# Attention and MLP in one kernel: in the first unit ACT's casts of x and of the heads are placed behind exponentials

## The chip, the cores and the metric

The kernel runs on one core of a Trainium2 chip. The metric is the device time of one execution in microseconds, the median of the runs shown. A profiled execution gives the rows below; its times are in microseconds from the start of its span.

Engine names: PE is TensorE (PEld its weight loads), ACT is ScalarE, DVE is VectorE, POOL is GpSimd, SP is SyncE, which issues the transfers (SPq is its queue).

## The reference

```python
scores = scale * np.matmul(q, k.transpose(0, 1, 3, 2))      # B=4, H=8, S=768, D=64
keep = is_sink | in_window                                  # first 4 keys, and the last 128
scores = np.where(keep, scores, -1000000000.0)
a = np.exp(scores - np.max(scores, axis=-1, keepdims=True))
a = a / (np.sum(a, axis=-1, keepdims=True) + 1e-09)
x = np.matmul(a, v)                                         # -> (3072 tokens, 512)
h = x @ w_in                                                # 512 -> 2048
g = np.maximum(0.01 * h, h)
out = (g @ w_out).astype(np.float32)                        # 2048 -> 512
```

## The kernel before, in words

The work is cut into eight units, one for each batch and half of its sequence, of 384 queries each. A unit has eight heads, taken in four pairs, and each head has three query blocks j = 0, 1, 2 of 128 rows. Only the keys of a block's window and the four sinks are multiplied.

One block goes through these steps. PE multiplies the scores into PSUM (L321, tile s). DVE adds the mask and takes the row's minimum of the negated scores (L341). ACT takes the exponential with its row sum (L345). DVE adds the small constant and takes the reciprocal of the sum (L346, L347) and scales the row into pk (L351). PE transposes pk (L376, tile t), and ACT copies the result to pt (L379). For unit 0 the transposes share a single PSUM tile, so a transpose waits for the copy of the one before it. When a pair is through, its sink columns are transposed too (L419), and PE multiplies pt by the values (L457, tile v). ACT rounds the result, x, to the matmul type as xh (L519, in emit_x), and DVE forms the rest xl (L520).

A head's queries and keys reach SBUF as qkraw. They are used in two parts, a rounded one and a rest: split_head has ACT cast qkraw into qksp (L278), and POOL then subtracts for the rest, in two instructions (L279, L281). Heads 0 and 1 of unit 0 are used unsplit. qksp has two buffers, so the cast for head h+2 waits until the scores of head h are done. The tag qkraw has one buffer, and in unit 0 the odd heads have one of their own, qkraw2. From unit 1 on every head uses qkraw, so there the transfer of a head can be issued only when POOL has finished the split of the head before. The calls are these:

```python
nxt = following(u, h)
if u < WIDE and j == min(nxt[0], 1):
    split_next(u, h)      # cast of the following head
```

So a head of unit 0 has its successor split right after its block 0, and head 7 of unit 0 has the first head of unit 1 split after its block 1.

The MLP of a unit runs one unit behind the attention. Its weights come as 64-bit words, which DVE packs to floats (L175, L177, L179), ACT rounds (L183: wih, woh) and POOL subtracts (L184: wil, wol). A step has twelve matmuls of h (L573), ACT's scaling (L580), DVE's maximum (L581), ACT's cast gh (L582), DVE's rest gl (L583), and nine matmuls of o (L594). There is one PSUM tile for h, so the next step's matmuls wait for the maximum.

PE's order is written out by the two streams of the program and stays as written, with short dummy matmuls in unit 0 (L311). The order on ACT, DVE, POOL and SP is chosen by a scheduler, which places each instruction where its own timeline finds it ready. Every engine takes its instructions in the order that results, and so does SP with its transfers.

## Time and profile before

| | us |
|---|---|
| median of 3 runs | 744.82 (744.72 to 745.72) |
| the profiled execution's own time | 745.67 |
| its span | 743.7 |
| PE busy | 718.4 |
| DVE busy | 562.2 |
| ACT busy | 433.3 |
| POOL busy | 381.3 |

The span is what the rows cover; the execution's own time has about 2 us around it. A busy time is the sum over an engine's instructions. The page's granted clock of PE is a share of full speed, 2.4 GHz; a half is the other level, 1.2 GHz.

### The profile page before, as it was taken

To read this page: it belongs to the slowest core of one execution; us is meant where nothing else is said; L and a number is where in the kernel's file an instruction comes from. 1 tells how busy PE (TensorE), PEld (TensorE's weight loads), DVE (VectorE), ACT (ScalarE), POOL (GpSimd) and SP (SyncE) were. 2 spreads that over 40 slices of the span, in tenths; PEclk is the share of its full clock that TensorE was granted. 3 is DMA by queue.
4 is the path that set the end of the run, shared out by engine and by line. 5 is a ranking of instruction groups with operands and counts; after the bars stand their busy time and mean duration, and the time that the engine had idled before them with its cause. 6 is when DMAs were issued, how large, how long until landed. Compare 5 with 4: busy or idle time off the path is not lost.

```text
span 743.7 us, 12694 instructions
## 1 busy us (share of the span) xinstructions
PE 718.4 (97%) x3935; PEld 623.0 (84%) x3935; DVE 562.2 (76%) x1832; ACT 433.3 (58%) x1208; POOL 381.3 (51%) x490
## 2 busy tenths in 40 slices
PE   8879999989999999999999999999999999999996
PEld 4547777769999988999988988999988999988995
DVE  7776889877667888888888888888888978733222
ACT  5567667657666566666566666666666655522221
POOL 3554455555445677665666577665666555300000
PEclk9989999999999999999999999999999999999998
DMA  6443565643121343324333343324331321001001
GB/s 209 163 133 125 187 203 189 186 141 100 58 57 62 115 125 122 90 92 154 115 108 109 130 125 109 98 93 150 120 107 49 107 69 44 1 1 42 1 1 46
DMA packets 30474, 76.94 MB, mean 103 GB/s; under 512 B 3584, under 2 KB 9152, under 8 KB 30400
## 3 DMA queue, kind: packets, MB, share of 16 engines
q1 hardware_dynamic: 30256, 75.94, 32.5%
q8 instruction: 33, 0.54, 0.3%
q14 instruction: 41, 0.34, 0.1%
q10 hardware_dynamic: 144, 0.13, 0.1%
HBM read 69.76 MB, written 6.29 MB: 102 GB/s over the span
## 4 chain that ended last, share of the span: by engine, by line
PE 83%; DVE 8%; ACT 5%; issue 2%; DMA 1%; POOL 1%; SPq 0%; ACTq 0%; DVEq 0%
PE o L594 32%; PE h L573 32%; PE v L457 9%; PE s L321 5%; PE t L389 2%; DVE gl L583 2%; PE warm L311 1%; PE t L376 1%; ACT qksp L278 1%; DVE zeroi L196 1%; ACT s L345 1%; DVE pk L351 1%; DMA qkraw<-in_qk 1%; DVE g L581 1%; ACT pk L345 0%
## 5 line engine op out<-in xcount | busy, mean ns | idle before, releaser
L573 PE MATMUL h<-xh,wih 128*128 128x384 f32 x512 | 187.6, 366 | 1.5 <-DVE g L581 1.3
L573 PE MATMUL h<-xh,wil 128*128 128x384 f32 x512 | 172.8, 338 | 1.5 <-POOL wil L184 1.5
L573 PE MATMUL h<-xl,wih 128*128 128x384 f32 x512 | 172.4, 337 | 0.0
L594 PE MATMUL o<-woh,gh 128*128 128x512 f32 x384 | 154.2, 402 | 0.0
L594 PE MATMUL o<-woh,gl 128*128 128x512 f32 x384 | 151.2, 394 | 0.0
L594 PE MATMUL o<-wol,gh 128*128 128x512 f32 x384 | 151.0, 393 | 0.0
L360 POOL TENSOR_SCALAR_AFFINE_SELECT pt<-stg 128x256 fp32r<-128x256 f32 x240 | 101.4, 447 | 83.3 <-DVE stg L402 67.8
L279 POOL TENSOR_TENSOR qksp<-qkraw,qksp 64x524 fp32r<-64x524 f32 (+1 forms) x62 | 74.9, 1208 | 112.9 <-issue 65.7
L583 DVE TENSOR_TENSOR gl<-g,gh 128x384 fp32r<-128x384 f32 x128 | 105.8, 827 | 17.3 <-ACT gh L582 15.8
L581 DVE TENSOR_TENSOR g<-h,g 128x384 f32<-128x384 f32 x128 | 71.0, 555 | 60.2 <-ACT g L580 58.0
L573 PEld LDWEIGHTS h<-xh,wih 128*128 128x128 f32 x512 | 96.5, 188 | 16.0 <-issue 2.9
L580 ACT ACTIVATE g<-h 128x384 f32<-128x384 f32 x128 | 62.2, 486 | 69.6 <-PE h L573 69.0
L345 ACT ACTIVATE pk<-pk,negm 128x128 f32<-128x128 f32 (+2 forms) x168 | 70.3, 418 | 55.7 <-DVE negm L341 54.7
L573 PEld LDWEIGHTS h<-xl,wih 128*128 128x128 f32 x512 | 96.9, 189 | 3.0
L573 PEld LDWEIGHTS h<-xh,wil 128*128 128x128 f32 x512 | 96.2, 188 | 1.8 <-POOL wil L184 1.8
L594 PEld LDWEIGHTS o<-woh,gl 128*128 128x128 f32 x384 | 72.0, 188 | 16.3 <-DVE gl L583 0.2
L582 ACT CAST gh<-g 128x384 fp32r<-128x384 f32 x128 | 65.7, 513 | 32.9 <-DVE g L581 30.6
L594 PEld LDWEIGHTS o<-woh,gh 128*128 128x128 f32 x384 | 72.4, 189 | 11.2 <-issue 2.4
L321 PEld LDWEIGHTS s<-qksp 128*128 128x128 f32 x372 | 68.8, 191 | 13.7 <-issue 5.0
L321 PE MATMUL s<-qksp 128*128 128x260 f32 (+1 forms) x372 | 77.1, 289 | 2.4 <-DVE negm L341 2.4
L594 PEld LDWEIGHTS o<-wol,gh 128*128 128x128 f32 x384 | 72.3, 188 | 6.5
L281 POOL TENSOR_TENSOR qksp<-qkraw,qksp 128x384 fp32r<-128x384 f32 x62 | 67.9, 1095 | 4.7
(124 smaller groups left out, 1218.8 us busy)
## 6 DMA issues: line engine op xcount, KB each, us to landing
qkraw<-in_qk SPq DMA_DIRECT2D x32, 454.0 KB, 3.2
qkraw<-in_qk SPq DMA_DIRECT2D x30, 388.0 KB, 3.5
wiraw<-in_w_in SPq DMA_DIRECT2D x16, 512.0 KB, 3.7
woraw<-in_w_out SPq DMA_DIRECT2D x16, 512.0 KB, 3.6
ciraw<-in_w_in SPq DMA_DIRECT2D x16, 512.0 KB, 3.5
coraw<-in_w_out SPq DMA_DIRECT2D x16, 512.0 KB, 3.6
out<-ob SPq DMA_DIRECT2D x23, 256.0 KB, 2.0
vraw<-in_vu SPq DMA_DIRECT2D x12, 256.0 KB, 2.6
```

The lines of the kernel that those rows point to most:

```text
L279: nc.gpsimd.tensor_tensor(out=sp[D:P, TU:TU + n], in0=raw[D:P, TU:TU + n], in1=sp[D:P, TU:TU + n].bitcast(F32), op=ALU.subtract)
L281: nc.gpsimd.tensor_tensor(out=sp[:, TU + n:2 * TU + n], in0=raw[:, 0:TU], in1=sp[:, 0:TU].bitcast(F32), op=ALU.subtract)
L321: nc.tensor.matmul(ps[:, 0:kn], lhsT=sp[rows, off + j * P:off + (j + 1) * P], rhs=sp[rows, TU + k0:TU + k0 + kn], start=c == 0, stop=c == ...
L345: nc.scalar.activation(out=e, in_=e, func=AF.Exp, scale=-1.0, bias=neg, accum_out=sm)
L360: nc.gpsimd.affine_select(out=out, in_=src, pattern=([[0, x]] if x > 1 else []) + [[sign, P]], base=-1 if prev else 0, channel_multiplier= ...
L457: nc.tensor.matmul(out[:, o:o + m], lhsT=l, rhs=r, start=c == 0, stop=c == len(mms) - 1, skip_group_check=True)
L573: nc.tensor.matmul(ph[:, 0:TU], lhsT=w[:, cs], rhs=x, start=cc == 0 and c == 0, stop=cc == NCC - 1 and c == 2)
L580: nc.scalar.mul(g, ph[:, 0:TU], 0.01)
L581: anchor[0] = nc.vector.tensor_tensor(out=g, in0=ph[:, 0:TU], in1=g, op=ALU.max)
L582: nc.scalar.copy(out=gh, in_=g)
L583: (nc.gpsimd if u == 0 and fc % 4 < GLP else nc.vector).tensor_tensor(out=gl, in0=g, in1=gh.bitcast(F32), op=ALU.subtract)
L594: nc.tensor.matmul(po[t], lhsT=gg[:, tsl], rhs=w, start=f == 0 and c == 0, stop=f == NFC - 1 and c == 2)
```

## The change

The program keeps a list of its exponentials. A helper, behind_exp, gives an instruction the rule that it may not stand ahead of a named earlier exponential on its engine. It is used for two casts. The cast of x (emit_x), in unit 0 alone, is placed behind the latest exponential that has been written. The cast of a head (split_head) is placed behind the one before the latest, while the program is in unit 0. Nothing is added to or removed from the work, and the rule itself is an order, not a wait.

```diff
--- before.py
+++ after.py
@@ -153,6 +153,7 @@
     mlp_steps = NFC * (NCC + T)
     wts = {}
     anchor = [None]
+    exps = []
 
     def raw_words(nm, fc, name):
         raw = iopool.tile([P, 512, 2], I32, tag="wraw", name=name, bufs=2)
@@ -269,13 +270,19 @@
             sps[nxt] = split_head(*nxt)
             pump()
 
+    def behind_exp(u, back, f):
+        if u == 0 and len(exps) >= back:
+            with tc.issue_after(exps[-back].ins):
+                return f()
+        return f()
+
     def split_head(u, h):
         half = u % 2
         n = NK[half]
         raw = raws.pop((u, h))
         rawbusy.discard(raw_place(u, h)[1])
         sp = apool.tile([P, 2 * TU + NK[1]], F32R, tag="qksp", name=f"qksp{u}_{h}")
-        nc.scalar.copy(out=sp[:, 0:TU + n], in_=raw[:, 0:TU + n])
+        behind_exp(phase["unit"], 2, lambda: nc.scalar.copy(out=sp[:, 0:TU + n], in_=raw[:, 0:TU + n]))
         nc.gpsimd.tensor_tensor(out=sp[D:P, TU:TU + n], in0=raw[D:P, TU:TU + n],
                                 in1=sp[D:P, TU:TU + n].bitcast(F32), op=ALU.subtract)
         nc.gpsimd.tensor_tensor(out=sp[:, TU + n:2 * TU + n], in0=raw[:, 0:TU],
@@ -342,7 +349,7 @@
                                                    scale=-SCALE, scalar=3.0e38, op0=ALU.add, op1=ALU.min,
                                                    accum_out=neg)
         sm = apool.tile([P, 1], F32, tag="sm", name=f"sm{u}_{h}_{j}", bufs=4)
-        nc.scalar.activation(out=e, in_=e, func=AF.Exp, scale=-1.0, bias=neg, accum_out=sm)
+        exps.append(nc.scalar.activation(out=e, in_=e, func=AF.Exp, scale=-1.0, bias=neg, accum_out=sm))
         nc.vector.tensor_scalar(out=sm, in0=sm, scalar1=1e-9, scalar2=None, op0=ALU.add)
         nc.vector.reciprocal(out=sm, in_=sm)
         if NACT >> u & 1:
@@ -516,7 +523,7 @@
     def emit_x(u, pair, x):
         xh = xpool.tile([P, TU], F32R, tag=f"xh{pair}", name=f"xh{u}_{pair}")
         xl = xpool.tile([P, TU], F32R, tag=f"xl{pair}", name=f"xl{u}_{pair}")
-        nc.scalar.copy(out=xh, in_=x)
+        behind_exp(u, 1, lambda: nc.scalar.copy(out=xh, in_=x))
         (nc.gpsimd if u < XLP and not native_values(u, 2 * pair) else nc.vector).tensor_tensor(out=xl, in0=x, in1=xh.bitcast(F32), op=ALU.subtract)
         xs[u].append((xh, xl))
```

The scheduler runs with these rules and orders the four engines anew; PE's order is unchanged. In the rows below, names end in numbers: s0_3_1 is unit 0, head 3, block 1, and the last number is a buffer's.

On ACT, around the cast of x of the first pair, the order before is this (xh0_0 is the cast of x, qksp0_5 that of head 5):

```order
L519 CAST xh0_0_382<-v0_0_342 128x384
L382 COPY sk0_1_259<-pk0_2_260 128x2x4
L278 CAST qksp0_5_417<-qkraw0_5_275 128x776
L345 ACTIVATE s0_3_0_349,sm0_3_0_353<-s0_3_0_349,negm_65 128x128
L379 COPY pt0_2_261<-t9_399 128x256
L345 ACTIVATE s0_3_1_369,sm0_3_1_373<-s0_3_1_369,negm_65 128x260
L345 ACTIVATE s0_3_2_390,sm0_3_2_394<-s0_3_2_390,negm_65 128x260
L379 COPY pt0_2_261<-t10_423 128x256
```

and with the change:

```order
L389 COPY sk0_1_259<-pk0_2_260 128x2x4
L352 ACTIVATE s0_3_0_349,sm0_3_0_353<-s0_3_0_349,negm_65 128x128
L386 COPY pt0_2_261<-t9_399 128x256
L352 ACTIVATE s0_3_1_369,sm0_3_1_373<-s0_3_1_369,negm_65 128x260
L526 CAST xh0_0_382<-v0_0_342 128x384
L386 COPY pt0_2_261<-t10_423 128x256
L352 ACTIVATE s0_3_2_390,sm0_3_2_394<-s0_3_2_390,negm_65 128x260
L285 CAST qksp0_5_417<-qkraw0_5_275 128x776
```

The cast of x has moved behind two exponentials of head 3 and a copy, and head 5's cast behind all three exponentials.

On ACT, at the end of unit 0, the twelve rows from the cast of unit 1's head 0 (qksp1_0) to that of its head 1 (qksp1_1) are these before:

```order
L278 CAST qksp1_0_662<-qkraw1_0_508 128x908
L345 ACTIVATE s0_6_2_601,sm0_6_2_605<-s0_6_2_601,negm_65 128x260
L379 COPY pt0_6_553<-t22_648 128x128
L183 CAST wih2_619<-wi2_614 128x512
L519 CAST xh0_2_672<-v0_4_632 128x384
L382 COPY sk0_3_551<-pk0_6_552 128x2x4
L345 ACTIVATE s0_7_0_639,sm0_7_0_643<-s0_7_0_639,negm_65 128x128
L379 COPY pt0_6_553<-t23_689 128x256
L345 ACTIVATE s0_7_1_653,sm0_7_1_657<-s0_7_1_653,negm_65 128x260
L345 ACTIVATE s0_7_2_680,sm0_7_2_684<-s0_7_2_680,negm_65 128x260
L379 COPY pt0_6_553<-t24_707 128x256
L278 CAST qksp1_1_732<-qkraw1_1_666 128x908
```

and with the change:

```order
L285 CAST qksp1_0_662<-qkraw1_0_508 128x908
L386 COPY pt0_6_553<-t23_689 128x256
L352 ACTIVATE s0_7_1_653,sm0_7_1_657<-s0_7_1_653,negm_65 128x260
L526 CAST xh0_2_672<-v0_4_632 128x384
L352 ACTIVATE s0_7_2_680,sm0_7_2_684<-s0_7_2_680,negm_65 128x260
L184 CAST woh2_628<-wo2_623 128x512
L386 COPY pt0_6_553<-t24_707 128x256
L389 COPY sk0_3_551<-pk0_7_637 128x2x4
L352 ACTIVATE pk1_0_696,sm1_0_0_702<-pk1_0_696,negm_65 128x260
L386 COPY pt0_7_638<-t25_714 128x128
L356 ACTIVATE pk1_0_696<-pk1_0_696,sm1_0_0_702 128x260
L285 CAST qksp1_1_732<-qkraw1_1_666 128x908
```

Head 0's cast stood ahead of the exponential of head 6, block 2, and now stands behind that of head 7, block 0. Head 1's cast stood ahead of the copy to pt0_7 from t25. It now stands behind that copy, and the next row behind it is the copy to pt0_7 from t26.

On SP, the transfers around qkraw1_1, which feeds that cast, are these before:

```order
L159 DMA wiraw3_676<-in_w_in 128x1024
L222 DMA qkraw1_1_666<-in_qk1 128x908
L246 DMA vn1_2_957<-in_vu1 128x512
L247 DMA vn1_2_957<-in_vs 24x128
L159 DMA woraw3_678<-in_w_out 128x1024
```

and with the change:

```order
L160 DMA wiraw3_676<-in_w_in 128x1024
L247 DMA vn1_2_957<-in_vu1 128x512
L248 DMA vn1_2_957<-in_vs 24x128
L160 DMA woraw3_678<-in_w_out 128x1024
L223 DMA qkraw1_1_666<-in_qk1 128x908
```

The transfer of head 1 was the second of these and is now the last, behind the weights woraw3.

On POOL, in unit 1, where the MLP has begun, the order before is this (wil6 is the rest of the weights of MLP step 6):

```order
L184 TENSOR_TENSOR wol5_1012<-wo5_1006,woh5_1011 128x512
L279 TENSOR_TENSOR qksp1_5_1277<-qkraw1_5_1128,qksp1_5_1277 64x524
L281 TENSOR_TENSOR qksp1_5_1277<-qkraw1_5_1128,qksp1_5_1277 128x384
L184 TENSOR_TENSOR wil6_1084<-wi6_1078,wih6_1083 128x512
L184 TENSOR_TENSOR wol6_1093<-wo6_1087,woh6_1092 128x512
L184 TENSOR_TENSOR wil7_1177<-wi7_1171,wih7_1176 128x512
```

and with the change:

```order
L185 TENSOR_TENSOR wol5_1012<-wo5_1006,woh5_1011 128x512
L185 TENSOR_TENSOR wil6_1084<-wi6_1078,wih6_1083 128x512
L286 TENSOR_TENSOR qksp1_5_1277<-qkraw1_5_1128,qksp1_5_1277 64x524
L288 TENSOR_TENSOR qksp1_5_1277<-qkraw1_5_1128,qksp1_5_1277 128x384
L185 TENSOR_TENSOR wol6_1093<-wo6_1087,woh6_1092 128x512
L185 TENSOR_TENSOR wil7_1177<-wi7_1171,wih7_1176 128x512
```

The rest wil6 has moved ahead of both subtractions of head 5.

## Rows read from the trace of the kernel before

**Rows 1.** Part 1 of the page: engine, busy us, share, instructions.
```profile
PE 718.4 (97%) x3935; PEld 623.0 (84%) x3935; DVE 562.2 (76%) x1832; ACT 433.3 (58%) x1208; POOL 381.3 (51%) x490
```

**Rows 2.** PE's timeline, unit 0: start, us, line, instruction, count, [idle before it <- releaser].
```profile
24.04 0.44 PE L376 MATMUL t<-ident,pk 128*128 128x128 f32 x2 [0.88 <-ACT pt L379]
...
26.12 0.30 PE L376 MATMUL t<-ident,pk 128*128 128x128 f32 x1 [1.32 <-ACT woh L183]
...
39.49 0.30 PE L376 MATMUL t<-ident,pk 128*128 128x128 f32 x1 [1.48 <-DVE sm L347]
...
51.98 0.30 PE L376 MATMUL t<-ident,pk 128*128 128x128 f32 x1 [1.51 <-DVE pk L351]
...
54.27 0.69 PE L376 MATMUL t<-ident,pk 128*128 128x128 f32 x2 [0.65 <-ACT pt L379]
...
60.93 0.45 PE L573 MATMUL h<-xh,wih 128*128 128x384 f32 x1
```

**Rows 3.** PE's timeline, later on.
```profile
65.03 0.44 PE L573 MATMUL h<-xh,wih 128*128 128x384 f32 x1 [1.27 <-DVE g L581]
...
117.06 0.44 PE L573 MATMUL h<-xh,wil 128*128 128x384 f32 x1 [1.45 <-POOL wil L184]
```

**Rows 4.** Windows of 2 us: busy us of each engine (instructions), then PE's granted clock, DMA.
```profile
26.00:28.00 2.00, 1.88 (x9) 1.43 (x9) 1.72 (x7) 0.76 (x4) 1.27 (x1) 0.63 0.86 240
28.00:30.00 2.00, 2.00 (x9) 1.27 (x7) 0.34 (x3) 0.96 (x4) 0.00 (x0) 0.52 0.58 229
```

**Rows 5.** ACT's timeline around the first cast of x, columns as in the second group.
```profile
22.05 0.48 ACT L519 CAST xh<-v 128x384 fp32r<-128x384 f32 x1 [1.52 <-PE v L457]
...
23.27 0.34 ACT L345 ACTIVATE s<-s,negm 128x128 f32<-128x128 f32 x1
...
23.62 0.36 ACT L379 COPY pt<-t 128x256 f32<-128x256 f32 x1
```

**Rows 6.** DVE's timeline, unit 0.
```profile
20.15 0.29 DVE L341 CUSTOM_DVE_ANT_0 s<-s,m 128x128 f32<-128x128 f32 x1
...
24.49 0.16 DVE L346 TENSOR_SCALAR sm<-sm 128x1 f32<-128x1 f32 x1 [0.23 <-ACT s L345]
...
25.64 0.73 DVE L351 TENSOR_SCALAR pk<-s,sm 128x128 f32<-128x128 f32 x2
...
46.62 0.29 DVE L341 CUSTOM_DVE_ANT_0 s<-s,m 128x128 f32<-128x128 f32 x1
...
50.69 0.68 DVE L179 SCALAR_TENSOR_TENSOR wo<-woraw,wod 128x512 int32<-128x512 int32 x1
```

**Rows 7.** ACT's timeline: casts of heads, and the first step of the MLP.
```profile
43.23 0.95 ACT L278 CAST qksp<-qkraw 128x908 fp32r<-128x908 f32 x1 [0.83 <-PE s L321]
...
51.17 0.95 ACT L278 CAST qksp<-qkraw 128x908 fp32r<-128x908 f32 x1 [0.33 <-DMA qkraw<-in_qk]
...
57.96 0.95 ACT L278 CAST qksp<-qkraw 128x908 fp32r<-128x908 f32 x1 [0.82 <-DMA qkraw<-in_qk]
...
63.51 0.50 ACT L349 ACTIVATE pk<-pk,sm 128x260 f32<-128x260 f32 x1
...
63.91 0.47 ACT L580 ACTIVATE g<-h 128x384 f32<-128x384 f32 x1
```

**Rows 8.** SP's queue: when it issues transfers (us is the issue alone).
```profile
46.33 0.33 SPq L159 DMA_DIRECT2D wiraw<-in_w_in  x1
...
46.77 0.37 SPq L222 DMA_DIRECT2D qkraw<-in_qk  x1
...
51.41 0.33 SPq L159 DMA_DIRECT2D woraw<-in_w_out  x1
...
54.65 0.33 SPq L222 DMA_DIRECT2D qkraw<-in_qk  x1
```

**Rows 9.** POOL's timeline around 115 us.
```profile
113.36 1.32 POOL L279 TENSOR_TENSOR qksp<-qkraw,qksp 64x524 fp32r<-64x524 f32 x1 [2.63 <-issue]
...
115.73 1.28 POOL L184 TENSOR_TENSOR wil<-wi,wih 128x512 fp32r<-128x512 f32 x1
```

## The prediction

> **What bounds the kernel now.** I read the page's busy times first, then PE's timeline from the start for its idle time, then the other engines' timelines back from each idle stretch. PE is busy for 97% of the span [rows 1]. The first matmul of the MLP starts at 60.93 [rows 2]. After it PE has work nearly all the time: its idle stretches of more than a microsecond are few, the two that matter here being 1.27 before 65.03 and 1.45 before 117.06 [rows 3]. So a microsecond won or lost ahead of 60.93 goes to the end one for one, and those two stretches are the places behind it where an order on another engine can still win something.
>
> Ahead of 60.93 PE stalls in the same way in each pair of heads. In the second pair (heads 2 and 3) it waits 0.88 before 24.04 for a copy, and 1.32 before 26.12 for the first scaled block of head 3. In the third pair the latter wait is 1.48, before 39.49, and in the fourth 1.51, before 51.98 [rows 2]. After these waits the clock falls: in the 2 us from 26 the granted clock is 0.63, and in the next 2 us 0.52, near the 1.2 GHz level, with PE busy for 1.88 and 2.00 of them [rows 4].
>
> Why head 3's block is late is seen on ACT. The cast of x waits 1.52 for PE and starts at 22.05. Behind it stands head 3's first exponential, which starts at 23.27 [rows 5], though DVE's mask for it ran at 20.15 for 0.29 [rows 6]. ACT sat idle in front of ready work.
>
> **The change, part by part.** It adds no instruction. All effects are those of order, so each term is how much later or earlier one PE instruction gets its input.
>
> *First two heads' part (to about 20 us).* Casts of heads 2 to 4 move by one or two exponentials. The scores that need them come later than the split in either order, since PE has transposes and dummies to do between. I cost this at nothing; if that cover fails, it costs about a cast, under 0.9.
>
> *Second pair.* The first exponential of head 3 can now run ahead of the cast of x. But PE's wait before 26.12 ends with DVE's scaling, which starts at 25.64 [rows 6], and DVE is busy with weights and masks in between. What goes is the 0.23 that it idles before 24.49 and the two small sums or reciprocals (0.16 each the one at 24.49 [rows 6]) that now stand behind the scaling: 0.23 + 0.2 or so. I take 0.45 earlier. The bounds are nothing and the whole 1.32.
>
> *Third pair.* The same pattern with the same order, so the same 0.45, with bounds of nothing and 1.48.
>
> *Fourth pair.* Here the order turns against the kernel. Head 0 of unit 1 was cast at 43.23 [rows 7]. It now stands behind the exponential of head 7, block 0. That exponential's mask runs at 46.62 for 0.29 [rows 6], so with reading out the minimum it can start near 47.0. An exponential of this size holds ACT for 23.62 - 23.27 = 0.35 [rows 5], so the cast starts at 47.35, 4.1 later. It takes 0.95 [rows 7], and POOL's two subtractions take 115.73 - 113.36 = 2.37 [rows 9], so the split is done at 50.7. Two things depend on it. Head 0's scores wait for it, some 1.3 longer, but that lies in the stall of 1.51 before 51.98, which stays where it was. The transfer of head 1 into the one qkraw buffer is the second: it was issued at 46.77 [rows 8], and now waits for POOL until 50.7 and for the weights woraw3, which are ahead of it on SP. Those were issued at 51.41, right after DVE's last packing (50.69 + 0.68 [rows 6]); the rest of x, half a microsecond, now stands behind that packing, so I put them at 51.0, and the transfer 0.44 later (46.77 - 46.33 [rows 8]), at 51.4.
>
> How long it takes is bounded by two rows. The one issued at 46.77, 0.44 behind 512 KB of weights, let its cast go at 51.17: 4.4. The one issued at 54.65, 3.24 behind such weights, let it go at 57.96: 3.3 [rows 7, 8]. The new place is like the first, so I take 4.4, and the cast starts at 55.8. The Trainium skill, page "DMA: Bandwidth & Descriptors", section "Queues, rings and completion order", says that each DMA engine consumes the descriptors of a queue in ring order. By that rule the transfer runs behind the weights, and the sum has 4.4 in it; with 3.3 the sum would be 1.1 lower. The two rows agree with it, though the order within an engine is not shown.
>
> The copy of head 7's second block stands directly behind that cast, and PE's last transpose of head 7, at 54.27 [rows 2], needs the copy, since the transposes share one tile. The cast ends at 56.75 and a copy takes 0.36 [rows 5], so the transpose starts at 57.15: **2.9 later**. The lower bound, with 3.3 for the transfer, is 1.8.
>
> *The first step of the MLP.* PE waits 1.27 before 65.03 for the maximum [rows 3], which waits for ACT's scaling at 63.91. A multiplication of 0.50 at 63.51 stands ahead of it [rows 7]; in the new order that one has gone ahead of an exponential that waits anyway. I take 0.35 earlier, between nothing and 0.4.
>
> *Step 6 of the MLP.* PE waits 1.45 before 117.06 [rows 3] for wil6, which POOL takes at 115.73 behind the split of head 5 at 113.36 [rows 9]. With wil6 first it can be done up to 2.37 sooner, which is more than the wait. I take all 1.45; if ACT's cast of those weights is late, nothing is won.
>
> *The clock.* The new stall in front of the transpose is longer, so PE comes back at the lower clock later, and value matmuls that ran at full clock fall into it. From the stretch at 26 us (1.88 and 2.00 busy at 0.63 and 0.52 [rows 4], so 1.88 x 0.37 + 2.00 x 0.48 = 1.7 lost against full clock at the most) I take 0.3 for the part that is new.
>
> The sum is -0.45 - 0.45 + 2.9 - 0.35 - 1.45 + 0.3 = +0.5. The profiled execution has 743.7 of span and 745.67 in all; it should become 744.2 of span. It is 0.85 above the median of the runs, 744.82, so the forecast is set on the median: **745.3**.
>
> **The rivals.**
>
> *The gain at step 6 does not come.* Another rest or cast is late in its place, or the wait moves to the next step. The order on POOL speaks against it, since the wait ends with that very instruction; that ACT and DVE are rearranged in all of unit 1 speaks for it. The sum is then +1.95: 746.8. It decides if PE still waits over a microsecond near 117.
>
> *The transfer is there in time.* Head 1's transfer takes 3.3, or the weights ahead of it are early, and the last transpose of head 7 loses 1.8 or less. The cast at 57.96, which waited only 3.3, speaks for it; the weights issued right ahead speak against. The sum is -0.6: 744.2.
>
> *The clock stays up.* This one ends on the fast side. If the waits before 26.12 and 39.49 shrink enough, the clock does not fall after them. The stretch at 26 loses at most 1.7 to the lower clock [rows 4]; since copies pace a part of it, I count 1.2 for each of the two pairs: 0.5 - 2.4 = -1.9, or 742.9. What speaks against it: in the new order the wait before 24.04 merely joins that before 26.12, and some 1.75 of their 2.2 is left. It decides if the granted clock between 26 and 30 stays at 1. The Trainium skill, page "TensorE: Matmul & The Clock Gate", section "HAM oscillation — how this bites in real kernels", says that idle stretches between bursts drop the clock, so that each burst starts cold. By that rule a shorter wait may keep it up; the drop behind the waits of today agrees.
>
> **How the numbers follow.** My forecast has a chance of 0.5, with its own range of 744.3 to 746.4. Step 6 without its gain has 0.25, the early transfer 0.13, the clock that stays up 0.12. The median can tell about 0.2%, 1.5 us, from no change: faster is below 743.3, slower above 746.3. The clock case is faster (0.12); most of the case without step 6 (0.21) and the upper tail of the forecast (0.04) are slower; the rest, 0.63, is within. The range runs from just above the clock case to just above that without step 6, 743.2 to 747.2, which leaves out about 0.2.
>
> **What would show it.** Right: the head cast that feeds unit 1's head 1 waits a few microseconds for its transfer, with a copy right behind it and PE idle for over 2 us ahead of the last transpose of unit 0; the waits like that before 26.12 start earlier by about half a microsecond; the first matmul of the MLP is about 2.3 later, near 63.2; no wait for a rest of weights near 117. Wrong: the MLP starts earlier than 60.93, which would mean that the blocked copy is not on the path; or the clock never falls in unit 0; or PE finds new waits of a microsecond in units 1 and 2, which I count at nothing.

## The result, and the profile after

The changed kernel takes 748.50 us in the median of 14 runs, where the kernel before takes 745.81 in runs beside it. The ratio is 1.0038, with a 95% interval of 1.0022 to 1.0053: slower by 2.7 us between the medians, and outside the predicted range of 743.2 to 747.2. The profiled execution took 747.95 with a span of 745.7; before it was 745.67 and 743.7. So its span is 2.0 longer, where the prediction's sum was +0.5. The medians here and below leave out two executions that were disturbed as a whole (794.46 of only_last, 1797.17 of copy34_wil9).

PE is busy for 2.9 us more than before at the same number of matmuls [rows 1]. From part 1 of the page of the changed kernel:

```profile
PE 721.3 (97%) x3935; PEld 623.2 (84%) x3935; DVE 564.5 (76%) x1832; ACT 434.1 (58%) x1208; POOL 381.3 (51%) x490
```

PE's timeline of the changed kernel: the waits of unit 0, the first matmul of the MLP, and the waits behind it that are new or smaller:

```profile
25.10 0.30 PE L383 MATMUL t<-ident,pk 128*128 128x128 f32 x1 [1.61 <-DVE sm L353]
...
37.87 0.30 PE L383 MATMUL t<-ident,pk 128*128 128x128 f32 x1 [1.61 <-DVE sm L353]
...
48.30 0.39 PE L328 MATMUL s<-qksp 128*128 128x260 f32 x1 [0.32 <-POOL qksp L286]
...
49.38 0.39 PE L328 MATMUL s<-qksp 128*128 128x260 f32 x1 [0.69 <-POOL qksp L288]
...
56.36 0.69 PE L383 MATMUL t<-ident,pk 128*128 128x128 f32 x2 [1.82 <-ACT pt L386]
...
63.37 0.44 PE L580 MATMUL h<-xh,wih 128*128 128x384 f32 x1
...
67.15 0.44 PE L580 MATMUL h<-xh,wih 128*128 128x384 f32 x1 [0.95 <-DVE g L588]
...
77.43 0.28 PE L426 MATMUL t<-ident,sk 128*24 128x128 f32 x1 [0.76 <-ACT pt L386]
...
101.64 0.28 PE L426 MATMUL t<-ident,sk 128*24 128x128 f32 x1 [0.66 <-ACT pt L386]
...
145.54 0.45 PE L580 MATMUL h<-xh,wil 128*128 128x384 f32 x1 [0.74 <-POOL wil L185]
```

Against [rows 2, 3]: the second pair's two waits, 0.88 and 1.32, have become one of 1.61, and the transpose behind it comes 1.0 sooner; in the third pair it comes 1.6 sooner. The last transpose of head 7, at 56.36, comes 2.1 later, and the first matmul of the MLP, at 63.37, 2.4 later. The wait of 1.45 at 117.06 is gone, but there are three waits of 0.66 to 0.76 that were not there.

PE takes its matmuls in the same order in both kernels, so the same matmul can be followed from one trace to the other. These mark the ends of further stretches, in the kernel before and then in the changed one (there, the fourth is the row at 48.30):

```profile
18.51 0.64 PE L457 MATMUL v<-sn,vn 16*64 16x256 f32 x2 [0.28 <-DVE sm L346]
...
31.81 0.64 PE L457 MATMUL v<-sn,vn 16*64 16x256 f32 x2 [0.48 <-DVE sn L423]
...
44.91 0.64 PE L457 MATMUL v<-sn,vn 16*64 16x256 f32 x2 [0.23 <-DVE sm L346]
...
49.10 0.53 PE L321 MATMUL s<-qksp 128*128 128x260 f32 x2
```
```profile
18.11 0.64 PE L464 MATMUL v<-sn,vn 16*64 16x256 f32 x2 [0.42 <-DVE sm L353]
...
30.87 0.64 PE L464 MATMUL v<-sn,vn 16*64 16x256 f32 x2 [0.37 <-DVE sm L353]
...
43.50 0.64 PE L464 MATMUL v<-sn,vn 16*64 16x256 f32 x2
```

The table gives the us from one such matmul to the next. The stretches are named by the times in the kernel before; the two further executions of the changed kernel are after_look1 and after_look2 below.

| stretch | before | changed | two further executions | change foretold |
|---|---|---|---|---|
| up to 18.51 | 18.51 | 18.11 | 18.28, 17.78 | none |
| second pair, 18.51 to 26.12 | 7.61 | 6.99 | 7.00, 7.00 | -0.45 |
| 26.12 to 31.81 | 5.69 | 5.77 | 4.80, 4.80 | none |
| third pair, 31.81 to 39.49 | 7.68 | 7.00 | 7.00, 7.00 | -0.45 |
| 39.49 to 44.91 | 5.42 | 5.63 | 5.50, 4.80 | none |
| to the scores of unit 1's head 0, 44.91 to 49.10 | 4.19 | 4.80 | 4.88, 4.88 | none |
| 49.10 to 51.98 | 2.88 | 2.81 | 2.80, 2.81 | none |
| to the last transpose of head 7, 51.98 to 54.27 | 2.29 | 5.25 | 5.06, 5.67 | +2.9 |
| to the MLP, 54.27 to 60.93 | 6.66 | 7.01 | 6.94, 7.42 | +0.3 |

ACT's timeline (columns as PE's), SP's queue and POOL's split of unit 1's head 0 show the last pair:

```profile
45.88 0.94 ACT L285 CAST qksp<-qkraw 128x908 fp32r<-128x908 f32 x1
...
55.09 0.95 ACT L285 CAST qksp<-qkraw 128x908 fp32r<-128x908 f32 x1 [1.09 <-DMA qkraw<-in_qk]
55.94 0.37 ACT L386 COPY pt<-t 128x256 f32<-128x256 f32 x1
```
```profile
50.16 0.33 SPq L160 DMA_DIRECT2D woraw<-in_w_out  x1
50.65 0.39 SPq L223 DMA_DIRECT2D qkraw<-in_qk  x1
```
```profile
46.95 1.30 POOL L286 TENSOR_TENSOR qksp<-qkraw,qksp 64x524 fp32r<-64x524 f32 x1
48.33 1.00 POOL L288 TENSOR_TENSOR qksp<-qkraw,qksp 128x384 fp32r<-128x384 f32 x1
```

The cast of head 0 comes at 45.88 (before 43.23 [rows 7]), so the split ends at 49.33. The transfer of head 1 is issued at 50.65, right behind the weights, and lands 4.4 later; its cast waits 1.09 for it; the copy behind the cast starts at 55.94, and PE's transpose at 56.36 waited for that copy. It is the chain that the prediction drew.

The windows of PE (busy us, granted clock, DMA) of the changed kernel, and then of the kernel before, at the end of unit 0:

```profile
50.00:55.00 5.00, 3.93 (x12) 0.50 0.60 203
55.00:60.00 5.00, 3.64 (x11) 0.50 0.10 20
60.00:65.00 5.00, 5.00 (x27) 1.00 0.21 76
```
```profile
50.00:55.00 5.00, 2.82 (x16) 0.88 0.56 191
55.00:60.00 5.00, 5.00 (x21) 0.78 0.30 93
60.00:65.00 5.00, 3.75 (x21) 1.00 0.31 95
```

In the changed kernel PE runs at the lower level, 1.2 GHz, all the way from 50 to 60.

The MLP goes by steps of twelve matmuls of its first layer. The distance from the first of these matmuls to the last of the whole run (60.93 to 732.14 before, 63.37 to 734.18 after) shrinks by 0.40 only, where the prediction had 1.80 for it (0.35 at the first step and 1.45 at a later one).

### The profile page after: what moved, and what is told of

The parts are those of the page before. It is cut to its first block, busy times and chain, and to the rows that moved or that the text cites. A ratio compares the mean times of both kernels' runs of the same rounds, so it can differ in the third digit from the quotient of the medians.

```text
span 745.7 us, 12701 instructions
## 1 busy us (share of the span) xinstructions
PE 721.3 (97%) x3935; PEld 623.2 (84%) x3935; DVE 564.5 (76%) x1832; ACT 434.1 (58%) x1208; POOL 381.3 (51%) x490
## 4 chain that ended last, share of the span: by engine, by line
PE 81%; DVE 11%; ACT 5%; issue 2%; DMA 1%; POOL 0%; ACTq 0%; SPq 0%; DVEq 0%; POOLq 0%
PE o L601 31%; PE h L580 31%; PE v L464 10%; PE s L328 5%; DVE gl L590 2%; PE t L396 2%; PE warm L318 1%; PE t L383 1%; ACT qksp L285 1%; DVE zeroi L197 1%; DVE pk L358 1%; DVE g L588 1%; DVE pk L348 1%; DMA qkraw<-in_qk 1%; ACT pk L352 1%
```

## The experiments

Fourteen runs, with medians beside runs of the kernel before on the same chip. "First" is the start of the first matmul of the MLP in the profiled execution (60.93 before), "rest" the distance from it to the last first-layer matmul (671.21 before).

| run | median | ratio to before (95%) | first | rest |
|---|---|---|---|---|
| the changed kernel | 748.50 | 1.0038 (1.0022 to 1.0053) | 63.37 | 670.81 |
| x_only | 745.15 | 0.9992 (0.9975 to 1.0009) | 58.88 | 671.82 |
| unit0_heads | 742.65 | 0.9957 (0.9937 to 0.9977) | 57.35 | 671.50 |
| only_last | 748.17 | 1.0036 (1.0019 to 1.0053) | 61.95 | 671.69 |
| cast_behind_copy | 745.43 | 0.9999 (0.9984 to 1.0015) | 59.65 | 670.69 |
| heads_only | 749.98 | 1.0055 (1.0034 to 1.0076) | 65.57 | 672.07 |
| own_buffer | 746.96 | 1.0015 (0.9997 to 1.0032) | 59.58 | 671.88 |
| copy34_first | 741.41 | 0.9943 (0.9924 to 0.9962) | 57.19 | 670.91 |
| copies_and_wil6 | 743.75 | 0.9964 (0.9946 to 0.9982) | 58.26 | 671.71 |
| wil9_only | 744.32 | 0.9981 (0.9959 to 1.0002) | 64.20 | 672.16 |
| unit0_heads_no_x | 744.42 | 0.9977 (0.9961 to 0.9992) | 59.01 | 672.25 |
| copy34_wil9 | 740.88 | 0.9926 (0.9900 to 0.9953) | | |
| copy34_wil9_b, the same kernel | 741.16 | 0.9943 (0.9927 to 0.9959) | 56.83 | 670.25 |
| after_look1, the changed kernel | 746.64 | one run | 62.26 | 670.80 |
| after_look2, the changed kernel | 747.25 | one run | 62.16 | 670.82 |

A start of the MLP in one execution carries the luck of the clock with it, as wil9_only shows below; verdicts on the time go by the medians. Where an expectation names 63.65 as the first matmul after the change, that is its second one; the first is 63.37.

**x_only: the cast of x alone.**

```diff
-        behind_exp(phase["unit"], 2, lambda: nc.scalar.copy(out=sp[:, 0:TU + n], in_=raw[:, 0:TU + n]))
+        nc.scalar.copy(out=sp[:, 0:TU + n], in_=raw[:, 0:TU + n])
```

> Only the cast of x is placed behind the latest exponential; the casts of heads are free, as before the change. Theory (the loss of the change is the late cast of unit 1's head 0, whose split lets the transfer of head 1 go): that cast stays near 43, the transfer is issued near 46.8 and PE's last transpose of head 7 is not late, so the first matmul of the MLP starts between 60.0 and 60.9 (before 60.93, after the change 63.65) and the time is equal to before or up to 1 us less. Rival (moving the cast of x is itself what costs, through the exponentials that go ahead of it): the MLP starts after 62 and the kernel is 2 us or more slower than before.

No loss: 745.15 beside 745.27. The rival falls; the cast of x is not what costs. The MLP began earlier than either expected, at 58.88. The clock may have a part in that, as it was 1.00 in all of 50 to 60 in this execution where before had 0.88 and 0.78; the median does not show a gain. Nor do the second and third pair, which take 7.78 and 7.55 here for 7.61 and 7.68 before.

**unit0_heads: the change without unit 1's heads.** The rule asks for the head's own unit, so the cast of unit 1's head 0 is free.

```diff
-        behind_exp(phase["unit"], 2, lambda: ...)
+        behind_exp(u, 2, lambda: ...)
```

> Both parts of the change, but the casts of unit 1's first heads, which are made while unit 0 runs, are left free. Theory (late cast of unit 1's head 0): cast near 43, transfer of head 1 issued near 46.8, the first matmul of the MLP near 60.1, that is 0.9 earlier than before by the second and the third pair of heads, which keep their gain of 0.45 each. The stall at step 6 of the MLP goes as in the changed kernel, since POOL takes that weight rest ahead of head 5. If unit 1 gets new waits as in the changed kernel (some 1.5), the end is about 0.9 earlier than before; if it gets none, 2.4 earlier. Rival (the waits and the low clock in the first pairs of heads make the loss, not the last pair): the MLP starts after 62 here too, and the kernel is slower than before by 2 us or more.

One word undone turns 2.7 us of loss into 2.6 of gain. The cast of head 0 runs at 41.14, the transfer of head 1 is issued at 44.76, and the last pair has only its own wait:

```profile
49.94 0.30 PE L383 MATMUL t<-ident,pk 128*128 128x128 f32 x1 [1.64 <-DVE pk L358]
...
52.90 0.28 PE L426 MATMUL t<-ident,sk 128*16 128x128 f32 x1 [0.26 <-ACT pt L386]
```

Its clock is 1.00 in 50 to 55 and in 55 to 60. The gain at the MLP's start, 3.6, is more than the 0.9 that I expected from the order. Followed by the same matmuls, 1.9 of it is won at waits: 0.6 in the second pair, 0.7 in the third, and 0.6 between 51.98 and 54.27, where the wait of 0.65 is gone. Another 1.6 lies in two stretches in which the kernel before is for a while at the low clock and this execution is not: 39.49 to 44.91 takes 4.79 for 5.42, and 54.27 to 60.93 takes 5.72 for 6.66. Of the rest of the run nothing is won: 671.50 against 671.21, with waits of 0.76, 0.67 and 0.74 like those of the changed kernel.

**only_last: only the cast of unit 1's head 0 is moved.**

```diff
-        behind_exp(phase["unit"], 2, lambda: ...)
+        behind_exp((phase["unit"] if u == 1 else 1), 2, lambda: ...)
...
-        behind_exp(u, 1, lambda: nc.scalar.copy(out=xh, in_=x))
+        nc.scalar.copy(out=xh, in_=x)
```

> Of the whole change only one thing is left: the cast of unit 1's head 0 is placed behind the latest exponential but one. Theory: this one cast makes the whole loss at the start. Cast near 46, transfer of head 1 issued near 51, the cast of head 1 waits about 1 us for it and ends near 56, PE's last transpose of head 7 at 56 to 57.2, and the first matmul of the MLP 2.4 to 3.3 later than before (63.3 to 64.2), since the second and third pair give nothing back. The end is then 1.5 to 3.5 later than before, depending on whether the stall at step 6 goes and new waits come in unit 1. Rival (the loss at the start is that of all moved casts together): the MLP starts less than 1 us later than before.

This one cast makes the kernel as slow as the whole change: 748.17. In ACT's timeline a copy stands behind the waiting cast again:

```profile
56.11 0.95 ACT L285 CAST qksp<-qkraw 128x908 fp32r<-128x908 f32 x1 [0.52 <-DMA qkraw<-in_qk]
56.96 0.36 ACT L386 COPY pt<-t 128x256 f32<-128x256 f32 x1
```

But here that copy reaches PE only as a wait of 0.97 before 57.38, behind the last transpose of head 7. Most of the loss comes earlier, where head 0's own scores wait for its late split:

```profile
50.57 0.39 PE L328 MATMUL s<-qksp 128*128 128x260 f32 x1 [2.47 <-POOL qksp L286]
51.64 0.39 PE L328 MATMUL s<-qksp 128*128 128x260 f32 x1 [0.69 <-POOL qksp L288]
```

The cast of head 0 runs at 47.98 in this run, 2.1 later than in the changed kernel, where the cast of x has moved too.

The first matmul of the MLP came at 61.95, only 1.0 later than before and not 2.4 to 3.3. The order of its first pairs is that of before, yet it was 1.4 ahead at the third pair's wait (38.11, where before has 39.49), since in this execution the clock did not fall behind the second pair's wait. The stretch from 26 to 30 in this run, and in the kernel before:

```profile
26.00:30.00 4.00, 3.81 (x22) 1.00 0.73 237
```
```profile
26.00:30.00 4.00, 3.88 (x16) 0.57 0.72 235
```

From the third pair's wait to the MLP it is 23.84 in this run and 21.44 before: 2.4 more, as expected in size. But 2.1 of it is there at the matmul of 51.98 already, ahead of the blocked copy, which the theory had as the cause.

**cast_behind_copy: the blocked copy goes first.** The split of unit 1's head 1 is written one block later, and its cast is placed behind the copy that PE waits for.

```diff
+    def place_cast(u, h, f):
+        if (u, h) == (1, 1):
+            with tc.issue_after(copies[-1].ins):
+                return f()
+        return behind_exp(phase["unit"], 2, f)
...
-            if u < WIDE and j == min(nxt[0], 1):
+            if u < WIDE and j == (2 if (u, h) == (1, 0) else min(nxt[0], 1)):
```

> The changed kernel, but the cast of unit 1's head 1, which waits for the late transfer, is put directly behind the copy that PE's last transpose of head 7 needs, not ahead of it. Theory (it is the copy queued behind the waiting cast that makes PE late): the last transpose of head 7 starts 1 to 1.8 earlier than in the changed kernel (56.36 there), and the first matmul of the MLP near 62 (63.65 there), and the end 1 to 1.8 earlier than in the changed kernel if unit 1 is not rearranged to its cost. Head 1's scores come later by a cast at most, which PE's first projection steps cover. Rival (the lateness of the transfer itself, or of head 0's split, holds PE, and the copy is only one of several things that come late): the first matmul of the MLP stays within 0.5 of 63.65.

The head 0 cast and the transfer stay late (issued at 48.83), but the copy no longer stands behind the cast, and the kernel is back at the time of before: 745.43. It is still 2.8 behind unit0_heads, so a part of the loss stays, and the gain of the second and third pair makes up for it. The first matmul of the MLP is 3.7 earlier than in the first profile of the changed kernel, 2.5 to 2.6 earlier than in the two further ones, where 1 to 1.8 was expected. ACT's and PE's timelines:

```profile
53.27 0.37 ACT L393 COPY pt<-t 128x256 f32<-128x256 f32 x1 [0.28 <-PE t L390]
53.54 0.95 ACT L292 CAST qksp<-qkraw 128x908 fp32r<-128x908 f32 x1
```
```profile
52.54 0.69 PE L390 MATMUL t<-ident,pk 128*128 128x128 f32 x2
```

The last transpose has no wait any more. From the transpose before it (the matmul of 51.98) it is 3.26, for 5.25 in the changed kernel and 2.29 before. So 2.0 of the loss is the copy queued behind the waiting cast, and the lateness of the transfer by itself does not hold PE. The part of the rival on head 0's split does not fall: 44.91 to 49.10 still takes 4.88 for 4.19.

**own_buffer: the transfer early, the order of the changed kernel.**

```diff
     def raw_place(u, h):
+        if (u, h) == (1, 1):
+            return apool, "vsp"
```

> The changed kernel, but the transfer of unit 1's head 1 goes into another buffer (the one of the values, free by then), so that it need not wait until head 0 is split. The late cast of head 0 stays. Theory (it is the late transfer, and the copy queued behind the cast that waits for it): the transfer is issued near 45 instead of 50.65, lands before its cast comes up, no copy waits behind the cast, and PE's last transpose of head 7 comes 1.5 to 2 sooner than the 56.36 of the changed kernel; the first matmul of the MLP starts near 61.5 to 62.2 (63.65 there), and the end is as much earlier. Rival (head 0's own late split, for which PE waits 1.0 in all before 49.38, and the low clock after it make the loss): the MLP starts within 0.6 of 63.65.

The other half of the chain. The transfer is issued at 45.98, the cast at 49.70 does not wait, and the last transpose runs at 53.41 without a wait. The first matmul of the MLP comes at 59.58, and the median is 746.96, 0.15% above that of before, with an interval that just holds 1. In unit 1 the order of before is back, with a stall of 1.46 for a weight rest, so the time does not measure the start alone. One copy does stand behind the cast, which the expectation did not have: PE waits 1.06 for it before 50.97. The waits of the changed kernel for head 0's split (0.39 and 0.69 here) are still there, and 44.91 to 49.10 takes 4.88 for 4.19; so they make a part of the loss, 0.7, but not the whole.

**heads_only: the casts of heads without that of x.**

```diff
-        behind_exp(u, 1, lambda: nc.scalar.copy(out=xh, in_=x))
+        nc.scalar.copy(out=xh, in_=x)
```

> Only the casts of heads are placed behind the latest exponential but one, that of unit 1's head 0 among them; the cast of x is free as before. Theory: unit 1's head 0 is late as in the changed kernel, the cast of head 1 stands ahead of a copy and waits for its transfer, so the last pair loses as much as in the changed kernel, while the second and third pair gain at most the half of what they gain with the cast of x moved too. The first matmul of the MLP is 2 to 4 later than before and the kernel 2 to 4 us slower. Rival (the cast of x makes a part of the loss): it is as fast as before.

Slower by some 4, the slowest of all: the last pair's loss without the gain of the cast of x. PE waits 2.46 for head 0's split before 50.35 and 1.69 for the blocked copy before 56.96, and the clock in its profile is 0.50 from 60 to 65 as well, which makes its first matmul (65.57, 4.6 late) later than expected.

**unit0_heads_no_x: the casts of unit 0's own heads alone.** The edits of unit0_heads and heads_only together.

> Only the casts of the first unit's own heads 4 to 7 are placed behind the latest exponential but one; the cast of x and the casts of unit 1's heads are free as before. It shows which part of the change brings the gain in the second and third pair. Theory (what PE waits for there is the first block of the odd head, whose exponential stands behind the cast of x, so the cast of x must move too): no gain, the waits before the second, third and fourth pair's odd head stay at 1.3 to 2, the first matmul of the MLP within 0.7 of before where the granted clock falls at the same places, and the time within 0.2 % of before. Rival (the casts of the heads alone are what was in the way): the MLP starts 1 us or more earlier, and the kernel is about as fast as with the cast of x moved too.

The two waits of the second pair join to one of 2.06 and do not shrink, as the theory has it (0.88 and 1.32 before [rows 2]), but the time is 0.2% below that of before, 0.9961 to 0.9992: a small gain that the theory did not have. With the cast of x alone there is no gain that shows, and with both it is 0.4%; whether that is more than the two together the intervals do not settle. The traces do, for the two pairs: the second and third pair take 7.62 and 7.62 here, 7.78 and 7.55 in x_only, and 7.0 each in all nine profiles with both casts moved. It takes both.

**copy34_first: one copy in unit 1.** On top of unit0_heads, the cast of the fourth step's weights is written behind the copy from t34.

```diff
+            if (nm, fc) == ("i", 4):
+                later[34] = cast
+            else:
+                cast()
...
+        if slots[0] in later:
+            with tc.issue_after(done_copy.ins):
+                later.pop(slots[0])()
```

> The version with unit 1's heads left free, and one thing more: in unit 1 the cast of the fourth step's weights on ACT is placed behind the copy of the last block of head 1, not ahead of it. Theory (in the changed kernel unit 1 lost its gain because copies stand behind work that waits for DVE): PE's wait of 0.76 for that copy, near 71.4 in that version, goes, and whatever follows from the new order of unit 1 comes as before the change: the wait of 0.67 near 96 goes too, and the stall of 1.45 at step 6 of the MLP is back, since POOL again splits head 5 ahead of that weight rest. From the first matmul of the MLP to the end the time is that of before within 0.4. Rival (those waits come from DVE, and the place of the copy on ACT does not matter): a wait of 0.5 or more stays at the sink transpose near 71.

In the changed kernel ACT has the copy that PE wants at 77.43 behind a multiplication and a weight cast that both wait for DVE, and the one wanted at 101.64 behind an exponential that does:

```profile
75.82 0.51 ACT L356 ACTIVATE pk<-pk,sm 128x260 f32<-128x260 f32 x1 [0.47 <-DVE sm L354]
76.49 0.62 ACT L184 CAST wih<-wi 128x512 fp32r<-128x512 f32 x1 [0.15 <-DVE wi L180]
77.01 0.37 ACT L386 COPY pt<-t 128x256 f32<-128x256 f32 x1
...
100.72 0.51 ACT L352 ACTIVATE pk<-pk,negm 128x260 f32<-128x260 f32 x1 [0.97 <-DVE negm L348]
...
101.23 0.35 ACT L386 COPY pt<-t 128x256 f32<-128x256 f32 x1
```

With the copy ahead, in copy34_first, it follows the multiplication at once, and PE does not wait:

```profile
69.66 0.51 ACT L364 ACTIVATE pk<-pk,sm 128x260 f32<-128x260 f32 x1 [0.47 <-DVE sm L362]
70.08 0.35 ACT L395 COPY pt<-t 128x256 f32<-128x256 f32 x1
70.33 0.62 ACT L188 CAST wih<-wi 128x512 fp32r<-128x512 f32 x1
```

The other wait went with it, since the order of all of unit 1 turned back to that of before, and the stall of 1.46 for a weight rest came back, at 112.99. All of it was expected. The kernel is 0.57% faster than before.

**copies_and_wil6: both copies first, and the weight rest first.** Two more placements on top, one of them this:

```diff
+        if (u, h) == (1, 5):
+            with tc.issue_after(whs["i", 6].ins):
+                return f()
```

> The version with unit 1's heads left free, and three placements on ACT in unit 1: the cast of the fourth step's weights behind the copy of head 1's last block, one exponential of head 4 behind the copy of head 3's last block, and the cast of head 5 behind the cast of the sixth step's weights, so that POOL takes that weight rest first. Theory (the new order of unit 1 gave 1.45 at step 6 and took about as much by copies behind waiting work): with both, the waits of 0.76 and 0.67 at the two sink transposes and the stall of 1.45 at step 6 are all gone, and from the first matmul of the MLP to the end it is 1 to 1.5 shorter than in the version with unit 1's heads left free, and the kernel some 4 us faster than before. Rival (each stall that is taken away comes back a step later, since ACT and DVE are full there): from the first matmul of the MLP to the end it is within 0.4 of that version.

Both waits for copies went, but the stall stayed:

```profile
114.85 0.44 PE L602 MATMUL h<-xh,wil 128*128 128x384 f32 x1 [1.45 <-POOL wil L190]
```

The rest of the run is 671.71, within 0.4 of unit0_heads as the rival has it, but the rival's reason was not put to the test, as no stall was taken away. The place was wrong. Counted in PE's timeline of before, nine whole steps of the MLP's first layer lie ahead of the stall: the rest that PE waits for there is that of step 9, and the split ahead of it on POOL is that of head 7. The prediction and the text ahead of it call them step 6, wil6 and head 5, whose order changes in the same way; the rows at 113.36 and 115.73 [rows 9] are of step 9.

**wil9_only: the right place, in the kernel before.**

```diff
+        if (u, h) == (1, 7):
+            with tc.issue_after(whs["i", 9].ins):
+                return f()
```

> The kernel before, with one thing changed: the cast of unit 1's head 7 on ACT is placed behind the cast of the ninth step's weights, so that POOL takes that weight rest (wil) ahead of the split of head 7. Nothing in the first unit moves. Theory (the stall of 1.45 before 117.06 comes from POOL's order, and the place is step 9 of the MLP, not step 6 as the prediction has it): PE's wait there goes, and if nothing else moves the end is 1.4 earlier than in the kernel before. Rival (what is taken away there comes back a few steps on, at one of the waits of 0.64 at 139 or 1.72 at 157): the time from the first matmul of the MLP to the end shrinks by less than 0.5.

The stall is gone. Followed by the same matmuls, PE is 4.46 behind the kernel before at the matmul of 114.98 and 3.66 at that of 123.05: 0.8 won, or 1.2 counted from just ahead of the stall, where the new order has already cost 0.4. But at 147 there is a new wait, and at the matmul of 149.99 it is 4.65 behind:

```profile
147.31 0.44 PE L580 MATMUL h<-xh,wil 128*128 128x384 f32 x1 [0.63 <-POOL wil L185]
```

At the last first-layer matmul it is 4.22, so 0.2 is left of the stall, as the rival has it. The median is 1.4 below before, with an interval that just holds 1. The profile shows something else that was not looked for. Up to 54.4 every wait of PE is that of before within 0.15, as the first unit is unchanged, but the first matmul of the MLP comes at 64.20, 3.3 later. In this execution the clock stayed low:

```profile
55.00:60.00 5.00, 5.00 (x15) 0.50 0.32 93
60.00:65.00 5.00, 5.00 (x14) 0.50 0.00 0
```

In the kernel before, the same stretches have 0.78 and 1.00.

**copy34_wil9 and copy34_wil9_b: the gains put together.** copy34_first with the edit of wil9_only, run twice; the rows are from the second.

> The version with unit 1's heads left free and the fourth step's weight cast behind the copy, with the cast of unit 1's head 7 behind the cast of the ninth step's weights as well. Theory: it keeps the gain of that version ahead of the MLP (first matmul 3 to 3.7 earlier than before) and takes the stall of 1.45 at step 9 away besides, so from the first matmul of the MLP to the end it is about 1.4 shorter than that version, and the kernel is 4 to 5.5 us faster than before, the fastest of all. Rival (the stall moves on to the later waits): no faster than that version, 741.4.

> The version with unit 1's heads left free, the fourth step's weight cast behind the copy and the cast of head 7 behind the ninth step's weights, once more for its profile. If a stall taken away at step 9 of the MLP is won for good, PE has no wait of over a microsecond near 112 and the rest of the run, from the first matmul of the MLP on, is 1.4 shorter than in the version without that last placement. If it comes back, as in the kernel where that placement alone was made (1.2 won by 123, 0.8 of it lost by 148), it is at most 0.5 shorter, and a new wait for a weight rest stands near 140.

740.9 and 741.2, the fastest kernel with copy34_first, which it does not beat by more than the measurement tells. In the profile the rest of the run is 670.25, 0.66 shorter than in copy34_first. PE is 0.36 ahead of copy34_first at the first matmul of the MLP, 1.2 ahead behind step 9, and only 0.43 ahead again at 142, behind this row:

```profile
138.38 0.44 PE L599 MATMUL h<-xh,wil 128*128 128x384 f32 x1 [0.60 <-POOL wil L190]
```

So the stall is paid back by 142. The 0.6 that is left comes at the end of unit 1, where copy34_first waits longer (first row) than this kernel (second row):

```profile
153.37 0.41 PE L335 MATMUL s<-qksp 128*128 128x128 f32 x2 [1.57 <-DVE negm L355]
```
```profile
152.27 0.41 PE L342 MATMUL s<-qksp 128*128 128x128 f32 x2 [0.77 <-DVE sm L368]
```

The two places go together: in all ten profiles with a wait of 0.60 to 0.75 for the weight rest of step 13, near 140, this one is 0.76 to 0.77, and in the five without it 1.53 to 1.88. The expectation had all of the stall won, or at most 0.5 of it.

**after_look1 and after_look2: the changed kernel again.**

> The changed kernel itself, another execution. If the low clock goes with the change, the granted clock is near 0.5 in all of 50 to 60 us again, the first matmul of the MLP starts within 0.5 of 63.65, and PE's waits are those of the first profile. If the clock is chance, it is up by 55 in one of the two executions and the MLP starts 1 to 2 sooner there, at the same waits.

> As in the execution before this one: low clock in all of 50 to 60 and a start of the MLP near 63.65 if it goes with the change; an earlier start at the same waits if it is chance.

The clock is 0.50 in 50 to 55 both times and 0.61 and 0.57 in 55 to 60. From after_look2:

```profile
50.00:55.00 5.00, 2.57 (x8) 0.50 0.46 169
55.00:60.00 5.00, 5.00 (x17) 0.57 0.30 93
```

So the low clock from 50 on goes with the change in all three profiles. Neither expectation fits whole: the MLP starts 1.1 and 1.2 sooner than in the first profile, but that is older, since at the third pair's wait (37.08 and 36.58, for 37.87) these executions are already 0.8 and 1.3 ahead. Their clock from 26 to 30 was 1.00, where the first profile has 0.59. The rest of the run is the same in all three: 670.81, 670.80 and 670.82.

## Why the prediction was wrong

**The last pair: the chain was right, its size too small.** Each link came as drawn: late cast, late split, transfer behind the weights, blocked copy, late transpose. only_last shows that this one cast is enough for the loss, and unit0_heads that without it there is none. The 4.4 for the transfer was measured as 4.4, and as 4.2 and 4.9 in the two further executions; that goes with the ring order that the prediction cites, but no run changes the place behind the weights alone. From the third pair's transpose to the last one of head 7 it is 14.78 before and 18.49 after (18.24 and 18.16 in the further executions), so the term is 3.4 to 3.7 and not 2.9.

Of these 3.7, the stretch with the blocked copy took 2.96 (2.8 and 3.4), as booked; cast_behind_copy shows 2.0 of it to hang on the place of the copy, and the other 1.0, in a stretch at the low clock, stays there when the copy goes first. What the term left out is the split of head 0 itself. The prediction has its wait lie in the stall of 1.51, at no cost; but 44.91 to 49.10 grew by 0.6 to 0.7 in all three executions, at a granted clock of 1.00, and only 0.1 of that was won back by 51.98. In only_last and heads_only, where the cast of x is free, this stretch takes 6.96, 2.8 more than before, and the split makes most of only_last's loss. cast_behind_copy and own_buffer, which cut the chain at two links, have 15.73 and 16.47 for the 18.49; a little over half of the 3.7 comes back in the second, and in the first three quarters, 0.8 of that in a stretch where the clock stayed up.

**The second and third pair: right in sign, too small.** The wait of 1.61 in place of two is the one left over that the prediction has (some 1.75). The two stretches are shorter by 0.62 and 0.68, for 0.45 each, and the clock has no part in it, as it was 1.00 throughout them. In the profile the third pair's transpose comes 1.6 earlier; besides these two, 0.4 of it was there at 18.51 already, where executions of the changed kernel differ by 0.5. All this makes up for the last pair: the transpose of head 7 is at 56.36, where the terms give 57.15 - 0.9 = 56.25. That the start of the MLP came at +2.44, for +2.3, is luck of errors that cancel; in the two further executions it is +1.33 and +1.23.

**The clock.** From the last transpose to the first matmul of the MLP it is 6.66 before and 7.01 after, 0.35 for 0.3. That it fits so well is luck as well: the order of before has 9.80 there in wil9_only, and the changed kernel 6.94 and 7.42 in its further executions. The clock is low from 50 on, ahead of the transpose too. That goes with the late cast of head 0, whether a copy is blocked or not: in the seven profiles that have it (three of the changed kernel, own_buffer, cast_behind_copy, only_last, heads_only) the granted clock from 50 to 60 is 0.50 to 0.83. With that cast free and others moved it is 1.00 in all six; in the order of before, 0.83 and 0.69. By the rule cited from the Trainium skill, page "TensorE: Matmul & The Clock Gate", section "HAM oscillation — how this bites in real kernels", idle stretches drop the clock. The longer stalls at the end of unit 0 agree, and unit0_heads, with a wait of 1.64 and one of 0.26 there, kept 1.00. The rival in which the clock stays up did not come in the changed kernel's first profile (0.59 from 26 to 30), though it did at that place in the two further ones, where 26.12 to 31.81 takes 4.80 for 5.77: 1.0, for the 1.2 that the rival counts.

**The first step of the MLP: right.** The wait went from 1.27 to 0.95: 0.32, for 0.35.

**Step 6 of the MLP: this is the step that failed.** The stall did go, and at its place it was worth what was booked and more: the changed kernel is 3.85 late ahead of it and 2.13 late behind it. But the sentence that new waits in units 1 and 2 are counted at nothing was wrong. The same new order put two copies on ACT behind work that waits for DVE. In PE's time (the start of the same matmuls, after minus before) the first step brings -0.32, the two copies +0.94 and +0.79, the stall -1.72, the late weight rest near 145 +0.53 (a wait of 0.64 just ahead of it is gone), and the end of unit 1 -0.73, where a wait of 1.72 has become one of 0.76. It adds up to -0.51, of which 0.1 is lost again over the rest of the run: 0.40 for an expected 1.80, and the same 0.4 in the two further executions. copy34_first shows that one of the copies and the weight rest hang on the same cast: with the copy ahead both waits for copies are gone and the stall is back. copy34_wil9_b shows that both can be had, and that the stall is then paid back at step 13, while the end of unit 1 gains 0.6. The rival "the gain at step 6 does not come" had the size (746.8), but not the way, since by its own test, a wait of over a microsecond near 117, it did not happen. That the place was named wrongly (step 9 and head 7) did not change the sum, as both places turn in the same way.

**The profile and the median.** With the 1.40 that the rest of the run did not give, the sum of +0.5 is +1.9, and the profile has +2.0. The median lies 0.55 above the first profiled execution of the changed kernel and 1.3 to 1.9 above the other two, while the one of before lies at its median. wil9_only shows how far executions of one order can part by the clock, and it may be that; but no execution of the changed kernel above 748 was profiled, so this part of the 2.7 stays open.

## What to carry to other kernels

When an order moves a cast that feeds a transfer, follow the buffer: the cast lets the buffer go, the buffer lets the transfer go, and the transfer's own cast may stand ahead of work that was ready. A rule of order is best put only where its reason holds; here the same rule with the head's own unit in place of the program's made the kernel 0.4% faster instead of 0.4% slower.

Where a scheduler orders engines anew, a gain that one reads off at one place is not to be booked alone: the same new order is at work everywhere, and the price is found by looking for each copy or cast that PE waits for, and what now stands ahead of it and waits itself. Where one engine keeps its order, follow the same instruction through both traces: a sum that fits can be made of terms that do not, and such stretches show each term by itself.

## What the runs showed of the hardware

After the same order and the same waits, PE's granted clock came back at different times in different executions: in the two halves of 55 to 65 it was 0.78 and 1.00 in one (the kernel before) and 0.50 and 0.50 in another (wil9_only), and the first matmul of the MLP was 3.3 us apart. The start of the MLP in one profiled execution is then no measure for a term below that size in this kernel. The distance between two of PE's matmuls is a better one, as long as the clock does not fall in between: from 18.51 to 26.12 it was 7.61 to 7.63 in three profiles with the order of before, and 6.99 to 7.00 in all nine with both casts moved. The distance from the first matmul of the MLP to the last one of its first layer repeated within 0.02 us in three executions of one program.
